# Loading the upper half of an expert weight from GpSimd's queue, and three idle products before a score product, in a fused mLSTM and MLP kernel

## The chip, the cores and the metric

The kernel runs on one core of a Trainium2 chip. A core has a matrix engine (TensorE, PE in the profile; its weight loads are the row PEld), three engines for elementwise work (VectorE or DVE, ScalarE or ACT, GpSimd or POOL), and a SyncE (SP) that does nothing here but issue transfers. Transfers between the chip's memory (DRAM) and the core's working memory (SBUF, 128 partitions) run on 16 DMA engines. Products of PE go to a small memory of their own, PSUM, in eight banks.

The metric is the time of one execution on the device in microseconds (us). A measurement of this kernel tells a difference of about half a per cent from none.

## The reference

Two stages, joined by a reshape. The first is an mLSTM cell, for 4 batches x 8 heads, 768 steps in time and a head width of 40:

```python
m_new  = np.maximum(f_gate[:, :, t] + m, i_gate[:, :, t])
f_stab = np.exp(f_gate[:, :, t] + m - m_new)
i_stab = np.exp(i_gate[:, :, t] - m_new)
C = f_stab * C + i_stab * np.einsum('bhd,bhe->bhde', vt, kt)
n = f_stab * n + i_stab * kt
h_tilde = np.einsum('bhde,bhe->bhd', C, qt)
denom = np.maximum(np.abs(np.einsum('bhd,bhd->bh', n, qt)), 1.0)
y[:, :, t] = sigmoid(o_gate[:, :, t]) * h_tilde / denom
```

Its output, read as 3072 tokens of 320 numbers, goes through an MLP with a leaky ReLU:

```python
h = x @ w_in                    # (3072, 320) @ (320, 2048)
g = np.maximum(0.01 * h, h)
out = g @ w_out                 # (3072, 2048) @ (2048, 320)
```

w_in and w_out arrive as 64-bit floating numbers; all other inputs are 32-bit. The kernel sees the weights as 64-bit words and makes 32-bit numbers of them itself.

## The kernel before

**Chunks and steps.** The 768 times are cut into 6 chunks of 128. A step is one chunk of one batch: step s has chunk s // 4 and batch s % 4, so there are 24. Within a chunk the recurrence is written as products: scores of q and k (`u_scores`), multiplied by a matrix `w` of exponentials of the gates (`spread_first`, `first_exps`, `next_exps`, `prep_mask`, `prep_exp`), times v (`u_values`), divided and gated (`gate`), turned to have channels on partitions (`u_x`), and a state that is carried on (`state`, `state_copy`, `state_next`). When the four steps of a chunk are done, its 512 tokens go through the MLP, in units that `ff_units` lists: `half(j, h)` (line 855) makes two blocks of 128 hidden channels for half of the tokens, `part` (877) sums the second product. From chunk 1 on the MLP runs in another form with fewer products (1019 and 912). The MLP of one chunk and the cell of the next are woven into one order.

**The order of work.** The program is written out by hand for PE, DVE, ACT and POOL: each of these engines does its instructions strictly in the order in which the Python code makes them. SP's transfers have an order of their own: class `Ordered` (line 90) chains every transfer of the first two chunks behind the one before it. `first_chunk` (line 1167) is the hand-written order of chunk 0 (steps 0 to 3) and of the loads that it and chunk 1 need; the loop behind it does the rest.

**The weights' way in.** w_in is loaded in four quarters of 512 columns (`load_weights`, line 236). A quarter has five blocks of 64 rows and stands in SBUF in two halves: partitions 0 to 63 hold the first 256 columns, partitions 64 to 127 the other 256. The order of the blocks is different in the two halves, 0 1 2 3 4 below and 1 2 3 4 0 above (`SLOTS`), so the lower half is one transfer and the upper half two, of four blocks and of one. Quarter 0 is loaded in two parts of 128 + 128 columns (`es`), the quarters 1 to 3 (`WHOLE`) in one. Every transfer of weights is issued by SP. They land as 64-bit words in places that are free for the moment: the quarters 0 and 1 at the end of the hidden activations (`acts`), the quarters 2 and 3 in `raw`. Quarter 0's parts and quarters 1 to 3 come in `first_chunk` and just behind it, between the loads of k, q, v and o of the steps 0 to 5, of a gate matrix that goes through DRAM (`a_dr`), and of w_out, which comes in eight loads over all 128 partitions.

`narrow_weights` (line 278) makes 32-bit numbers of a half quarter in six steps: two on ACT (lines 300, 301) and four on DVE (302, 305, 308, 309). They are taken from generators (`w`, `w1`, `n0`, `n1`) one or two at a time with `run`, so that they stand between other work. ACT's first step waits for the transfers of both halves.

**What POOL does in chunk 0.** Preparing tiles (memsets, `prepare_tiles`, `prepare_step`) and `prep_vu` (540, 544), v multiplied by a gate, which `state` needs. Before the change it issues no transfers.

**Scores of a step.** `u_scores(s)` takes two PSUM banks and makes 8 products of 40 rows from kqT, which ACT or DVE copied out of a transposing product (638); DVE then multiplies them into `w` (651). `warm` (367) and `u_x(1)` (841) hold products of an identity with itself whose results nobody reads.

Of the kernel before, what the change touches and what calls it, by code (L numbers as in the profile page):

```python
# [12 lines left out]
U64 = mybir.dt.uint64  # L13
# [6 lines left out]
def kernel(  # L20
# [26 lines left out]
    nc = tc.nc  # L47
    B, H, S, D = q.shape
    P = 128
# [5 lines left out]
    DP = 64  # L55
# [10 lines left out]
    NF = FF // P  # L66
    GT = B * P
    KF = Dm // P
    KR = Dm - KF * P
    KC = Dm // DP  # L70
# [102 lines left out]
    def prepare_tiles():  # L173

        for u in range(2):
            nc.gpsimd.tensor_copy(cm2[ts(u, SL)], cmask[ts(u, SL), ts(u, SL)])
        nc.gpsimd.memset(xb[:], 0.0)
        for t in rb_t:
            nc.gpsimd.memset(t[:, :, RL:], 0.0)

    def prepare_step(n):

        nc.gpsimd.memset(S_v[n][:SL, 0, :, :, DB:], 2.0)
        nc.gpsimd.memset(S_v[n][SL:, 1, :, :, DB:], 2.0)
        nc.gpsimd.memset(S_t[n][QW:SL, 1], 0.0)
# [3 lines left out]
    QN = NF // 4  # L189
    QC = 4 * P  # L190
# [40 lines left out]
        yield nc.vector.tensor_tensor(t2, a22, a12, op=ALU.subtract)  # L231
        yield nc.vector.tensor_tensor(t4, a21, t2, op=ALU.subtract)

    WHOLE = (1, 2, 3)

    def load_weights(n, es=(0, 1)):

        m = n - QN
        if n < QN:
            dst = w_in[:, n, :]  # L240
        else:
            dst = w_out[:, 2 * m : 2 * m + 2, :].rearrange("p a d -> p (a d)")
        to = dst
        if wide:
            if n < 2:
                at = NF * GT - 2 * WC * (n + 1)
                raw = acts_l[:, at : at + 2 * WC].bitcast(U64)
            elif n < QN:
                raw = raw_t[:, WC * (n - 2) : WC * (n - 1)]
            elif m < 2:  # L250
                raw = w_out[:].rearrange("p f d -> p (f d)")[:, (2 + m) * WC : (3 + m) * WC].bitcast(U64)
            else:
                at = (4, 0, 1, 2, 3, 4)[m - 2] * HW
                raw = raw_t[:, at : at + HW]
            raws[n] = (raw, dst)
            to = raw
        if n < QN:
            src = moe_w_in[:, n * QC : (n + 1) * QC].rearrange("(k p) (r c) -> r p k c", p=DP, r=2)
            halves = to.rearrange("p (e k c) -> p e k c", e=2, k=KC)
            both = to.rearrange("p (k c) -> p k c", k=KC)  # L260
            if n in WHOLE:
                es = es[:1] if es[0] == 0 else ()
            for e in es:
                for r in range(2):
                    at = 0
                    while at < KC:
                        k0, n_k = run_of(r, at)
                        if n in WHOLE:
                            rows, part = both[DP * r : DP * (r + 1), at : at + n_k], src[r, :, k0 : k0 + n_k, :]
                        else:  # L270
                            rows, part = halves[DP * r : DP * (r + 1), e, at : at + n_k], src[r, :, k0 : k0 + n_k, ts(e, P)]
                        sync.dma_start(rows, part)
                        at += n_k
        else:
            rows = moe_w_out[2 * m * P : 2 * (m + 1) * P, :]
            sync.dma_start(to.rearrange("p (a d) -> p a d", d=Dm), rows.rearrange("(a p) d -> p a d", p=P))

    def narrow_weights(n, e=None):

# [220 lines left out]
    def first_exps(ab, s2):  # L500

        w = w_all[:, s2 : s2 + 2].rearrange("p n (m r t) -> p n r m t", r=RG, t=P)
        for r in range(RG):
            nc.scalar.activation(w[:, :, r], ab[r][:], AF.Exp)

    def next_exps(ab, s2):

        for r in range(RG):
            for n in range(2):
                for m in range(H // RG):  # L510
                    h = m * RG + r
                    bh = (s2 + n) * H + h
                    yield nc.scalar.activation(  # L513
                        st[s2 + n]["w"][:, h, :], ab[r][:, n, m, :], AF.Exp, bias=gT[0][:, 0, bh : bh + 1], scale=1.0,
                    )
# [16 lines left out]
    def prep_vu(s):  # L532

        c, b = divmod(s, B)
        d = st[s]
        if s < NS:
            d["vu"] = wk.tile([P, H, 2, V1], F32, name="vu")
            g = gT[c][:, 1, ts(b, H)].unsqueeze(2).unsqueeze(3)
            if c == 0:
                nc.gpsimd.tensor_tensor(  # L540
                    d["vu"][:, :, :, :DB], d["va"][:, :, :D].rearrange("p h (k d) -> p h k d", d=DB),
                    g.to_broadcast([P, H, 2, DB]), op=ALU.mult,
                )
                nc.gpsimd.tensor_tensor(
                    d["vu"][:, :, :, DB], d["va"][:, :, D : D + 2], gT[c][:, 1, ts(b, H)].unsqueeze(2).to_broadcast([P, H, 2]),
                    op=ALU.mult,
                )
            else:
                d["ku"] = d["vu"][:].rearrange("p h k d -> p (h k d)")[:, : H * D].rearrange("p (h d) -> p h d", d=D)
                nc.gpsimd.tensor_tensor(  # L550
                    d["ku"], d["k"][:, :, :D], gT[c][:, 1, ts(b, H)].unsqueeze(2).to_broadcast([P, H, D]), op=ALU.mult,
                )
# [87 lines left out]
    def u_scores(s, between=()):  # L640
        d = st[s]
        kqT, w = d["kqT"], d["w"]
        sc = [psc.tile([P, PR, P], F32, name=f"sc{r}", tag="c") for r in range(2)]
        for j in range(PR):
            for r in range(2):
                rows = slice(DP * r, DP * r + D)
                nc.tensor.matmul(
                    sc[r][:, j, :], lhsT=kqT[rows, 0, ts(j, P)], rhs=kqT[rows, 1, ts(j, P)], start=True, stop=True,
                )
        for r in range(2):  # L650
            nc.vector.tensor_tensor(w[:, r::2, :], w[:, r::2, :], sc[r][:], op=ALU.mult)
            for fn in between if r == 0 else ():
                fn()
# [461 lines left out]
    def run(steps, n=None):  # L1115

        for _ in range(H if n is None else n):
            next(steps, None)
# [48 lines left out]
    def first_chunk():  # L1167

        for n in range(2):
            for i in range(3):  # L1170
                load_first(n, i)
        for n in range(2):
            load_first(n, 3)
        load_weights(0, (0,))
        on_v, on_s = nc.vector.tensor_copy, nc.scalar.copy
        gates(0)
        gates_exp(0)
        load_fi(2)
        warm(6)
        ab = spread_masks()  # L1180
        bu, a, _ = bus[0]
        spread_first(ab, a, bu, 0)
        gates_T(0, bu)
        prep_vu(0)
        first_exps(ab, 0)
        u_transpose(0, (on_v, on_v))
        u_scores(0)
        u_transpose(1, (on_s, on_s))
        ab = spread_masks()
        gates(1)  # L1190
        u_scores(1)
        prep_vu(1)
        prepare_tiles()
        e = next_exps(ab, 2)
        w, w1 = narrow_weights(0, 0), narrow_weights(0, 1)
        n0, n1 = narrow_weights(1, 0), narrow_weights(1, 1)
        ffs = []
        prep_o(0)
        prep_o(1)
        u_values(0)  # L1200
        gate(0)
        spread_first(ab, a, None, 2)
        u_values(1)
        load_first(2, 0)
        load_first(2, 1)
        load_weights(0, (1,))
        load_first(3, 0)
        load_first(3, 1)
        load_first(2, 2)
        load_first(3, 2)  # L1210
        load_first(2, 3)
        load_first(3, 3)
        load_weights(1, (0,))
        load_weights(1, (1,))
        run(e, 6)
        u_x(0)
        gate(1)
        run(w, 2)
        run(w, 4)
        u_x(1)  # L1220
        state(0)
        state(1)
        state_copy(0)
        state_copy(1)
        prepare_step(0)
        prepare_step(1)
        run(e, 2)
        ffs = ff_units(0)
        u_transpose(2, (on_s, on_s))
        run(e, 4)  # L1230
        gates_exp(1)
        run(w1, 2)
        run(e, 4)
        ffs[0]()
        run(w1, 2)
        prep_vu(2)
        prep_vu(3)
        u_scores(2)
        u_transpose(3, (on_v, on_s))
        run(w1, 2)  # L1240
        u_gates(1)
        u_scores(3)
        prep_o(2)
        prep_o(3)
        u_values(2)
        ffs[1]()
        gate(2)
        u_values(3)
        gate(3)
        u_x(2)  # L1250
        state(2)
        u_x(3)
        state(3)
        state_copy(2)
        run(n0, 4)
        state_copy(3)
        run(n0, 2)
        run(n1, 6)
        prepare_step(2)
        prepare_step(3)  # L1260
        return ffs

    E = mybir.EngineType
# [158 lines left out]
```

## Time and profile before

| | |
|---|---|
| median of three runs | 475.43 us (474.78 to 477.28) |
| the profiled execution's own time | 475.09 us |
| span of that execution on the core | 473.3 us |
| busy: PE, PEld | 463.5 us (98%), 418.0 us (88%) |
| busy: DVE, ACT, POOL | 338.6 (72%), 204.1 (43%), 171.3 (36%) |
| transfers issued by SP (queue q1) | 51.20 MB in 121,088 packets |
| transfers issued by ACT (queue q10) | 7.21 MB in 40,128 packets |
| mean granted clock of PE | 0.996 |

The page cuts the span into 40 equal slices of 11.8 us; a digit is the busy share of a slice in tenths. A wait is told as the instruction that waited, an arrow, and what it waited for, with the total, the number of times and the longest. In the timeline a row has its start, its duration, the engine, the line of the program, the operation, the tiles (written <- read), the number of instructions, and in brackets the idle time ahead of it. Matrix products of 32-bit numbers appear as two records each. Where a row names SPq, ACTq or POOLq, it is the time in which that engine issues a transfer and not the time of the transfer.

### The profile page before, as it was taken

To read this page: it belongs to the slowest core of one execution; us is meant where nothing else is said; L and a number is where in the kernel's file an instruction comes from. 1 tells how busy PE (TensorE), PEld (TensorE's weight loads), DVE (VectorE), ACT (ScalarE), POOL (GpSimd) and SP (SyncE) were. 2 spreads that over 40 slices of the span, in tenths; PEclk is the share of its full clock that TensorE was granted. 3 is DMA by queue.
4 is the path that set the end of the run, shared out by engine and by line. 5 is a ranking of instruction groups with operands and counts; after the bars stand their busy time and mean duration, and the time that the engine had idled before them with its cause. 6 is when DMAs were issued, how large, how long until landed. Compare 5 with 4: busy or idle time off the path is not lost.

```text
span 473.3 us, 14138 instructions
## 1 busy us (share of the span) xinstructions
PE 463.5 (98%) x5723; PEld 418.0 (88%) x5723; DVE 338.6 (72%) x607; ACT 204.1 (43%) x497; POOL 171.3 (36%) x205
## 2 busy tenths in 40 slices
PE   7998989999999999999999999999999999999997
PEld 6777878767788899988899988999988999988997
DVE  3868689999679989878688867788847786105531
ACT  3756878755337411367311366311456311253210
POOL 4330577274335154923214923214822005300020
PEclk9989999999999999999999999999999999999999
DMA  9999998886741595965754765753875103100001
GB/s 118 173 176 175 220 193 239 203 173 129 158 132 50 150 166 125 194 141 122 176 121 106 182 133 129 188 115 76 186 153 129 54 25 82 56 1 2 8 8 42
DMA packets 161281, 59.31 MB, mean 125 GB/s; under 512 B 123904, under 2 KB 152640, under 8 KB 161216
## 3 DMA queue, kind: packets, MB, share of 16 engines
q1 hardware_dynamic: 121088, 51.20, 48.7%
q10 hardware_dynamic: 40128, 7.21, 9.3%
q8 instruction: 45, 0.74, 0.7%
q14 instruction: 20, 0.16, 0.1%
HBM read 51.68 MB, written 6.70 MB: 123 GB/s over the span
## 4 chain that ended last, share of the span: by engine, by line
PE 89%; DMA 4%; ACT 3%; DVE 1%; SPq 1%; issue 1%; POOL 0%; DVEq 0%; POOLq 0%; ACTq 0%
PE ph L1019 33%; PE po L912 33%; PE po L877 8%; PE pT L794 3%; PE sd L706 3%; PE ph L855 3%; DMA raw<-in_moe_w_in_dram 3%; DMA acts<-in_v_dram 1%; SPq L96 1%; PE sd L712 1%; PE ab L495 1%; PE hN L766 1%; ACT w L513 1%; PE warm L367 1%; ACT w_in L300 1%
## 5 line engine op out<-in xcount | busy, mean ns | idle before, releaser
L912 PE MATMUL po<-w_out,acts 128*128 128x160 f32 x640 | 89.1, 300 | 0.0
L912 PEld LDWEIGHTS po<-w_out,acts 128*128 128x128 f32 x640 | 87.3, 190 | 0.6 <-ACT acts L1044 0.3
L1019 PE MATMUL ph<-xT,w_in 64*128 64x256 f32 x720 | 82.8, 378 | 0.0
L1019 PEld LDWEIGHTS ph<-xT,w_in 64*128 64x128 f32 x720 | 69.6, 187 | 8.3 <-issue 0.6
L1048 DVE TENSOR_TENSOR acts<-acts,ph 128x512 f32<-128x512 f32 x60 | 38.5, 683 | 40.3 <-PE ph L1019 40.3
L912 PE MATMUL po<-raw,acts 128*128 128x160 f32 x480 | 66.4, 300 | 0.0
L912 PEld LDWEIGHTS po<-raw,acts 128*128 128x128 f32 x480 | 65.4, 190 | 0.3
L1052 ACT COPY acts<-ph 128x512 f32<-128x512 f32 x60 | 32.2, 589 | 49.7 <-PE ph L1019 49.7
L522 POOL TENSOR_TENSOR w<-w,i 128x512 f32<-128x512 f32 x20 | 31.2, 1570 | 53.5 <-DMA w<-a_dr 26.5
L1044 ACT ACTIVATE acts<-acts 128x1024 f32<-128x1024 f32 x30 | 31.6, 1057 | 41.5 <-DVE acts L1048 33.7
L682 POOL TENSOR_TENSOR S<-S,f 40x336 f32<-40x336 f32 x36 | 31.3, 870 | 47.3 <-PE pT L794 31.8
L530 ACT ACTIVATE w<-w,gT 128x64 f32<-128x64 f32 x160 | 41.6, 340 | 12.1 <-DMA a_dr<-a 5.5
L723 DVE TENSOR_TENSOR qn<-w,sd 64x384 f32<-64x384 f32 (+1 forms) x80 | 33.4, 418 | 13.5 <-ACT acts L1052 7.8
L855 PE MATMUL ph<-xT,w_in 64*128 64x256 f32 x320 | 39.5, 395 | 1.1 <-DVE w_in L309 0.8
L855 PEld LDWEIGHTS ph<-xT,w_in 64*128 64x128 f32 x320 | 32.7, 194 | 5.5 <-DVE w_in L309 1.0
L877 PE MATMUL po<-w_out,acts 128*128 128x320 f32 x128 | 36.7, 437 | 0.0
L1019 PE MATMUL ph<-acts,w 64*128 64x256 f32 x320 | 36.3, 379 | 0.0
L808 POOL TENSOR_TENSOR xb<-xb,den 128x320 f32<-128x320 f32 x16 | 11.7, 729 | 67.2 <-DVE xb L805 62.5
L1019 PEld LDWEIGHTS ph<-acts,w 64*128 64x128 f32 x320 | 30.6, 187 | 3.6
L877 PEld LDWEIGHTS po<-w_out,acts 128*128 128x128 f32 x128 | 23.5, 190 | 9.2 <-ACT acts L863 0.3
L950 POOL TENSOR_TENSOR y<-y,raw 128x160 f32<-128x160 f32 x10 | 9.6, 958 | 59.5 <-ACT y L949 59.5
L595 DVE TENSOR_TENSOR qn<-kqT,ea 64x512 f32<-64x512 f32 x32 | 30.0, 938 | 0.8
(179 smaller groups left out, 734.6 us busy)
## 6 DMA issues: line engine op xcount, KB each, us to landing
rb<-in_k_dram SPq DMA_DIRECT2D x64, 80.0 KB
rb<-in_q_dram SPq DMA_DIRECT2D x64, 80.0 KB
rb<-in_o_gate_dram SPq DMA_DIRECT2D x64, 80.0 KB
ea<-a_dr SPq DMA_DIRECT2D x32, 128.0 KB
raw<-in_moe_w_out_dram SPq DMA_DIRECT2D x6, 640.0 KB
w<-a_dr ACTq DMA_DIRECT2D x24, 128.0 KB
x_dr<-x SPq DMA_DIRECT2D x64, 40.0 KB
xT<-x_dr SPq DMA_DIRECT2D x16, 160.0 KB
```

The source lines that it names most:

```text
L522: nc.gpsimd.tensor_tensor(w, w, cm2.unsqueeze(1).to_broadcast([P, H, SL]), op=ALU.add)
L530: yield nc.scalar.activation(w[:, h, :], w[:, h, :], AF.Exp, bias=gT[c][:, 0, bh : bh + 1], scale=1.0)
L595: nc.vector.tensor_tensor(mixed(s)[rows, 1 - r], d["kqT"][rows, 1].rearrange("p (h t) -> p h t", t=SL), d["ea"][rows], op=ALU.mult,)
L682: nc.gpsimd.tensor_tensor(new, old, g, op=ALU.mult)
L723: nc.vector.tensor_tensor(mixed(s)[toks, u, hs], w[toks, hs], bank[1 - u][to[u][hs.start], hs], op=ALU.mult,)
L855: nc.tensor.matmul(ph[r][:, cols], lhsT=w_row(r, slot, j), rhs=xT[DP * r : DP * (r + 1), slot, cols], start=(slot == 0), stop=(slot == KC ...
L877: nc.tensor.matmul(po[n][:], lhsT=acts[:, f, ts(n, P)], rhs=w_out[:, f, :], start=(f == 0), stop=(f == NF - 1),)
L912: nc.tensor.matmul(bank[:], lhsT=left[:, f, :], rhs=right[:, f, :], start=f == 0, stop=f == KH - 1)
L1019: nc.tensor.matmul(bank[r][:, e, :], lhsT=left(r)[rows, e], rhs=right(r)[rows], start=first and e == 0 and m == 0, stop=e == 1 and m == le ...
L1044: nc.scalar.activation(to, z, AF.Prelu, alpha=0.01)
L1048: nc.vector.tensor_tensor(to[:, 2 * r : 2 * r + 2], to[:, 2 * r : 2 * r + 2], bank[r], op=ALU.add)
L1052: nc.scalar.copy(to[:, 2 * r : 2 * r + 2], bank[r])
```

## The change

The upper half of every quarter of w_in is no longer issued by SP but by POOL, with the same two transfers of four blocks and of one (`load_upper`). They stand at written places in POOL's order: the two parts of quarter 0 behind `prep_vu(0)` and `prepare_tiles`, quarter 1 behind `prep_vu(2)`, quarter 2 behind `prep_vu(3)`, quarter 3 behind `prepare_step(3)`, the end of `first_chunk`. SP keeps the lower halves, in their places. `u_scores(3)` begins with three products of the identity with itself, into the first of its two banks, which the score products overwrite. `state_copy(3)` stands ahead of all six steps of `n0` where it stood behind four of them; two of these four are DVE's.

```diff
-    WHOLE = (1, 2, 3)
+    WHOLE, UPPER = (1, 2, 3), (0, 1, 2, 3)
+
+    def raw_of(n):
+
+        if n < 2:
+            at = NF * GT - 2 * WC * (n + 1)
+            return acts_l[:, at : at + 2 * WC].bitcast(U64)
+        return raw_t[:, WC * (n - 2) : WC * (n - 1)]
...
             for e in es:
-                for r in range(2):
+                for r in range(1 if n in UPPER else 2):
...
+    def load_upper(n, e=None):
+
+        src = moe_w_in[:, n * QC + QC // 2 : (n + 1) * QC].rearrange("(k p) c -> p k c", p=DP)
+        if e is None:
+            both = raw_of(n)[DP:].rearrange("p (k c) -> p k c", k=KC)
+        else:
+            both, src = raw_of(n)[DP:].rearrange("p (e k c) -> p e k c", e=2, k=KC)[:, e], src[:, :, ts(e, P)]
+        nc.gpsimd.dma_start(both[:, : KC - 1], src[:, 1:])
+        nc.gpsimd.dma_start(both[:, KC - 1 :], src[:, :1])
...
         sc = [psc.tile([P, PR, P], F32, name=f"sc{r}", tag="c") for r in range(2)]
+        for _ in range(3 if s == 3 else 0):
+            nc.tensor.matmul(sc[0][:, 0, :], lhsT=ident[:], rhs=ident[:], start=True, stop=True)
...
         prep_vu(0)
+        load_upper(0, 0)
...
         prepare_tiles()
+        load_upper(0, 1)
...
         prep_vu(2)
+        load_upper(1)
         prep_vu(3)
+        load_upper(2)
...
         state_copy(2)
-        run(n0, 4)
         state_copy(3)
-        run(n0, 2)
+        run(n0, 6)
         run(n1, 6)
         prepare_step(2)
         prepare_step(3)
+        load_upper(3)
```

More of the change, by code (lines that the diff above doesn't have):

```diff
@@ L244, in load_weights @@
         if wide:
[L245 to L249, printed above, removed]
+            if n < QN:
+                raw = raw_of(n)
             elif m < 2:
```

## The prediction

> **What bounds the kernel now.** The first view is the page's busy shares and slices.
>
> ```profile
> PE 463.5 (98%) x5723; PEld 418.0 (88%) x5723; DVE 338.6 (72%) x607; ACT 204.1 (43%) x497; POOL 171.3 (36%) x205
> ...
> PEclk9989999999999999999999999999999999999999
> DMA  9999998886741595965754765753875103100001
> GB/s 118 173 176 175 220 193 239 203 173 129 158 132 50 150 166 125 194 141 122 176 121 106 182 133 129 188 115 76 186 153 129 54 25 82 56 1 2 8 8 42
> ```
>
> TensorE (PE) works 463.5 of 473.3 us, so the kernel ends sooner only by what PE loses. It loses in two places: in idle, nearly all of it early, and in slice 3 (24 to 36 us), where the granted clock fell. The DMA engines are full in the same 70 us and half empty after. The second view is PE's own waits over the whole span, the third PE's timeline from 20 to 40 us.
>
> ```profile
> PE sc L647 <- DVE kqT L638: 1.7, 2, 0.9
> PE warm L367 <- POOL ident masks.py:199: 1.5, 1, 1.5
> PE sd L712 <- POOL vu L550: 0.9, 1, 0.9
> PE ph L855 <- DVE w_in L309: 0.8, 1, 0.8
> PE tk L621 <- DMA kn<-in_k_dram: 0.8, 1, 0.8
> PE xt L843 <- DVE x L754: 0.5, 1, 0.5
> PE ph L855 <- ACT acts L863: 0.3, 1, 0.3
> PE tk L621 <- DMA rb<-in_q_dram: 0.3, 1, 0.3
> ```
>
> ```profile
> 22.78 2.43 PE L855 MATMUL ph<-xT,w_in 64*128 64x256 f32 x20 [0.77 <-DVE w_in L309]
> ...
> 28.43 1.16 PE L647 MATMUL sc<-kqT 40*128 40x128 f32 x16 [0.75 <-DVE kqT L638]
> 29.52 1.13 PE L741 MATMUL pa<-S,w 128*64 128x41 f32 x32
> 30.58 4.12 PE L855 MATMUL ph<-xT,w_in 64*128 64x256 f32 x20
> ```
>
> The waits end at 70.3 us; from there to the last output PE has no gap. So whatever PE gains before 70 us reaches the end one for one, if nothing swallows it. The last row is the same work as the first and took 4.12 instead of 2.43 us: 1.69 us lost to the clock. The fourth view, windows, gives per stretch the busy time of PE, PEld, DVE, ACT and POOL, then the clock, the DMA share and GB/s.
>
> ```profile
> 14.00:14.50 0.50, 0.50 (x12) 0.47 (x10) 0.47 (x4) 0.10 (x1) 0.50 (x4) 1.00 0.95 324
> 30.50:31.00 0.50, 0.50 (x8) 0.42 (x6) 0.50 (x2) 0.00 (x0) 0.50 (x3) 0.75 1.08 344
> 31.00:32.50 1.50, 1.50 (x10) 1.20 (x8) 1.42 (x6) 0.00 (x0) 1.10 (x4) 0.50 1.08 203
> 37.00:40.00 3.00, 2.64 (x35) 2.30 (x37) 1.76 (x6) 2.17 (x5) 0.00 (x0) 1.00 1.05 196
> 57.50:59.00 1.50, 1.50 (x98) 1.43 (x92) 0.00 (x0) 1.25 (x5) 0.00 (x0) 1.00 1.04 388
> 64.50:65.50 1.00, 1.00 (x13) 0.89 (x11) 0.02 (x1) 0.98 (x3) 0.87 (x2) 1.00 1.01 407
> ```
>
> w_out, loaded over 128 partitions, streams at 388 and 407 GB/s; w_in, loaded over 64 partitions at a time, at 196 and 203 with the engines just as busy. Only where one half ends and the other begins (14.0, 30.5) do w_in's packets reach 324 and 344. So it is the half that is slow, not the source.
>
> **The transfers.** A quarter of w_in is 320 x 512 x 8 bytes, 1.31 MB; four make 5.24 MB. At 200 GB/s they hold the DMA engines 26 us; with both halves in flight at 390 they would hold them 13. Lower halves stay on SP, ten transfers leave it, and everything behind them on SP (k, q, v of steps 2 to 7, the gates' rows, w_out) goes out sooner. One write changes its place on SP: a_dr<-bu (72.17) goes out behind a w_out load (74.61), some 3 us later. Its first reader, ea<-a_dr, goes out at 90.17, so I cost it at nothing.
>
> What PE lost to transfers: 0.76 for kn of step 4 (46.56 us); 0.35 at 52.53 (ACT stood 1.53 us for raw of quarter 2, then was late with L863); 0.28 for rb of step 5 (63.08); 0.95 at 70.33 for vu of step 5, whose chain on POOL began with 7.67 us of waiting for w<-a_dr at L522. Sum 2.34. I let all of it go: at 46 us three quarters are in, 19.7 us of transfer at 200 GB/s, and if half of that overlaps the transfers are some 5 us ahead, more than PE's own lead (1.69 plus what it gained so far, at most 4). What is late next at 70 us is POOL's chain behind DVE's x (L774, 64.07): L779, L780, L559, L682, L550 take 0.72, 0.71, 1.39, 0.89, 0.85, which ends at 68.7, in time for 69.4.
>
> **POOL's new work.** Ten transfers are issued by POOL, and no row shows what one costs it. Nearest rows: SP's issue of the same w_in transfers, 0.61 us at the least, and one of 3.42 us where the queue was full. I take 1.4, between the median 0.62 and the 2.14 that is the longest into acts: 2.8 a pair, 14 in all, where POOL is 36% busy.
> - Upper 0, first half: POOL is free at 9.98; issued by 12.8, 256 KB and 64 KB in 1.6 us, there by 15 to 16; ACT's L300 wants it at 19.00. vu of step 1 moves from 12.83 to 13.8; PE wants it at 20.6.
> - Upper 0, second half: behind prepare_tiles (1.7 us), issued by 18.3, there by 20.5; wanted at 24.52.
> - Upper 1: behind vu of step 2, which waits for v until 27.86 at the latest. Issued by 31.6, 3.2 us of transfer, there by 34.8; wanted at 38.53, or 36.84 without the slow clock. vu of step 3 moves from 30.9 to 33.2; PE wants it at 36.4.
> - Upper 2 by 36.0, there by 41; wanted at 45.59. Upper 3 behind prepare_step(3), by 40, there by 45; wanted at 59.46. POOL's next work, L413, waits until 47.08 in any case.
> All five land in time as long as a pair stays under 4.9 us: 9.98 + d + 0.95 + 1.7 + d + 2 = 24.52, with 1.6 us of transfer in the 2. As bounds: nothing up to there, and at 3.42 each (6.8 a pair) 3.8 us at L300.
>
> DVE shares time with POOL: L309 took 0.83 us alone and 1.68 beside POOL. The second half of upper 0 is written beside gate(0) and gate(1) on DVE (L750 to L755), where PE has 0.2 us to spare. 0 to 1.0 us; I take 0.4.
>
> **The products.** Three 128x128 products at L841's pace (four in 1.06 us) take 0.80 us. They fill the 0.75 us in which PE waits for kqT, and their PSUM bank is free at 27.68, when L651 has read it: 0.05 us more. They also fill the stretch judged before the slow clock. That lasted from 30.75 to 34.16, 3.41 us; the stretch of that length before it held the 0.75 us gap and the thin products of 40 rows and 41 columns. If the filling keeps the clock up, 1.69 go. A gap of 0.77 at 22 us cost no clock, so a gap alone doesn't decide; the thin products do count, and 0.8 us of dense work is 23% of that stretch. The bounds are 0 and 1.69 and I take 1.69.
> The Trainium skill, "TensorE: Matmul & The Clock Gate", the table "Why this matters for your kernels", asks only that no idle of about 3 us stands between bursts. The trace differs: the clock fell behind a gap of 0.75. By that rule the products would keep nothing and the sum would be 473.2.
>
> **state_copy of step 3 ahead of two steps of quarter 1's narrowing.** It takes 0.68 us of DVE's idle 1.12 before L302 (39.37) and leaves L308 0.68 earlier; PE wants that weight at 43.2 and it is done at 42.9. Nothing, and less danger.
>
> **Sum.** The profiled execution took 475.09 (span 473.3 and 1.8 around it), 0.34 below the median 475.43. 475.09 - 2.34 - 1.69 + 0.05 + 0.4 = 471.5.
>
> **Rivals.**
> - Two halves don't overlap. Then transfers end as before, PE arrives 1.69 us sooner and waits that much longer for kn at 46.56: 475.1, or 474.6 because kn no longer stands behind the upper half on SP. For it: the bursts at 14.0 and 30.5 last only half a microsecond. Against it: they reach 324 and 344. The Trainium skill, "SBUF — State Buffer", section "Can I just issue two DMAs to hit both halves?", says no: two such transfers gained 6% over one. By that rule 475; the trace's bursts disagree as far as they go.
> - The clock falls all the same, there or elsewhere, as every arrival shifts: 471.5 + 1.69 = 473.2.
> - Slower: POOL writes its transfers too slowly. Place: L300 at 24.52, where ACT's exponentials and kqT of step 3 stand behind it. From 4.9 us a pair on, twice the excess. At 6.8: upper 0 is 3.8 us late, PE idles and the clock falls once more; 475.09 + 3.8 + 0.4 - 2.34 = 477.0 with a clock loss as before. For it: DVE is busy nearly all the time at 9 to 37 us and POOL's L540 went from 0.72 to 1.40 beside it. Against: it takes four times SP's 0.62. The Trainium skill, "SBUF — State Buffer", section "SBUF: two separate sides", warns that descriptors of a transfer issued by GpSimd can't be written while DVE holds the port they share; no run here shows it yet.
>
> **How the numbers follow.** Forecast 0.57 (own range 470.4 to 472.9), clock falls 0.12, no overlap 0.15, POOL too slow 0.16. A measurement tells about 0.5%, 2.4 us, from no change: faster is below 473.05. Forecast nearly all below (0.54) and half the clock case (0.06): 0.60 faster. The rest of these and no overlap: 0.24. POOL: 0.16. The range runs from 470.0 (the sum without the 0.4 for DVE and without the 0.77 at 22.78, 470.3, and 0.3 for scatter) to 476.0, which leaves out most of the slow case and a little below: 0.2.
>
> **What would show it.** Forecast: GB/s near 350 where quarters 1 and 2 load; no PE wait on kn or rb; clock 1.00 at 30 to 34 us; ph at 30.6 in 2.4 us. Overlap wrong: w_in still at 200 GB/s and kn waiting. POOL wrong: rows on POOL's queue over 2.4 us, and ACT's L300 waiting for transfers at 24 us. What would make the sum wrong is a chain that I call hidden, DVE from 75 to 124 us above all (94% busy), which has 0.7 us on PE at L309 (83.0).

## The result, and the profile after

The changed kernel takes 477.70 us in the median of 20 executions (475.55 to 478.97); the kernel before took 475.62 beside it (473.91 to 477.67, 20 executions). The ratio is 1.0036, with a 95% interval from 1.0025 to 1.0048: slower by a third of a per cent, 1.7 us, less than the half per cent that the prediction set as its bound and clearly not zero. The forecast was 471.5 with a range to 476.0, so it was wrong in sign. The profiled execution of the changed kernel took 477.64 us.

From here on line numbers are those of the changed kernel; what stood at 621, 712 and 855 before stands at 635, 728 and 871. First its page: busy shares, clock and transfers in 40 slices of 11.9 us.

```profile
span 475.8 us, 14162 instructions
...
PE 463.8 (97%) x5729; PEld 417.1 (88%) x5729; DVE 337.6 (71%) x607; ACT 203.8 (43%) x497; POOL 176.9 (37%) x215
...
PEclk9998999999999999999999999999999999999999
DMA  9999999976651584965664765753775203100001
GB/s 123 168 167 215 191 189 235 204 165 131 149 142 36 147 175 113 199 142 120 162 142 91 187 134 126 191 126 71 180 148 118 81 15 84 57 0 2 8 8 41
...
q0 software_dynamic: 800, 2.62, 2.6%
```

PE has the same work as before and a span 2.5 us longer. POOL's queue (q0) moved half of w_in, 2.62 MB, as the change says. The dip of the clock has moved from slice 3 to slice 4. The fourth slice moves 215 GB/s where it moved 175, the fifth 191 where it moved 220; the 350 that two halves in flight were to bring stands nowhere.

PE's waits, and its timeline from the products to step 4:

```profile
PE tk L635 <- DMA kn<-in_k_dram: 1.1, 1, 1.1
PE dC L678 <- issue: 1.1, 1, 1.1
PE sc L663 <- DVE kqT L652: 0.9, 1, 0.9
PE tkq L649 <- ACT xT L860: 0.7, 1, 0.7
...
PE ph L871 <- ACT acts L879: 0.6, 1, 0.6
PE ph L871 <- DVE w_in L323: 0.4, 1, 0.4
```

```profile
29.02 0.94 PE L659 MATMUL sc<-ident 128*128 128x128 f32 x6
29.89 1.16 PE L663 MATMUL sc<-kqT 40*128 40x128 f32 x16
30.98 1.13 PE L757 MATMUL pa<-S,w 128*64 128x41 f32 x32
32.04 2.43 PE L871 MATMUL ph<-xT,w_in 64*128 64x256 f32 x20
...
37.82 0.27 PE L678 MATMUL dC<-vu,kn 128*40 128x42 f32 x3
39.15 0.46 PE L678 MATMUL dC<-vu,kn 128*40 128x42 f32 x13 [1.05 <-issue]
39.54 8.43 PE L871 MATMUL ph<-xT,w_in 64*128 64x256 f32 x60
49.03 0.25 PE L635 MATMUL tk<-ident,kn 64*40 64x64 f32 x2 [1.06 <-DMA kn<-in_k_dram]
```

The products do what was forecast: the MLP's product at 32.04 takes 2.43 us instead of 4.12. But PE is late before that (its first MLP product starts at 23.80 and not at 22.78), and the gain does not last. PE pauses 1.05 us ahead of 39.15, meets a slow clock there, and reaches step 4 at 49.03 where the kernel before reached it at 46.56, still waiting for kn. The waits for vu and rb of step 5, 1.23 us before, are gone, and the lag shrinks to 0.85 us at 76.68 (hN, L782, before at 75.83). Behind that it grows again, to 1.6 at 92 and some 2 at 111. The narrowing of w_out on DVE stands in PE's waits there, and other runs, shown at the end, tell how this goes with the waits that are gone.

The windows, columns as in the prediction (busy times, clock, DMA share, GB/s):

```profile
30.00:32.00 2.00, 2.00 (x48) 1.87 (x48) 1.97 (x4) 0.94 (x2) 1.98 (x4) 1.00 0.96 214
32.00:34.00 2.00, 2.00 (x22) 1.78 (x20) 1.93 (x8) 0.00 (x0) 1.89 (x5) 1.00 1.14 217
34.00:36.00 2.00, 2.00 (x43) 1.61 (x39) 1.30 (x6) 0.72 (x3) 0.85 (x4) 1.00 1.11 202
36.00:38.00 2.00, 1.54 (x27) 1.07 (x24) 1.89 (x6) 1.14 (x4) 1.54 (x3) 1.00 1.07 196
38.00:40.00 2.00, 0.95 (x18) 0.80 (x17) 0.30 (x2) 1.10 (x3) 0.00 (x0) 0.91 1.03 234
40.00:42.00 2.00, 2.00 (x12) 1.61 (x10) 1.89 (x5) 2.00 (x4) 0.00 (x0) 0.50 1.04 281
```

From 30 to 38 us the engines move 196 to 217 GB/s, the pace of one half in the kernel before, and for much of that time only one half is in flight: from 30 to 32 POOL's queue moves nothing, and from 33 to 36 it moves 0.54 of the 0.65 MB. From 38 to 42 both queues carry a half. Their packets, MB and share of the 16 engines in these 4 us:

```profile
q0 software_dynamic: 180, 0.64, 60.8%
q1 hardware_dynamic: 277, 0.39, 42.8%
```

Together that is 258 GB/s: more than one half alone, and far from 390. POOL's own rows, and two of ACT's that stood at 13.63 and 14.53 before with waits of 0.25 and 0.43 us:

```profile
9.37 0.79 POOL L289 DMA_DIRECT2D acts<-in_moe_w_in_dram  x1
10.15 0.54 POOL L290 DMA_DIRECT2D acts<-in_moe_w_in_dram  x1
...
36.38 0.63 POOL L289 DMA_DIRECT2D raw<-in_moe_w_in_dram  x1
37.00 0.54 POOL L290 DMA_DIRECT2D raw<-in_moe_w_in_dram  x1
```

```profile
14.91 0.47 ACT L580 ACTIVATE raw<-raw 128x320 f32<-128x320 f32 x1 [2.15 <-DMA raw<-in_o_gate_dram]
17.52 0.47 ACT L580 ACTIVATE raw<-raw 128x320 f32<-128x320 f32 x1 [2.14 <-DMA raw<-in_o_gate_dram]
```

A pair costs POOL 1.2 to 1.3 us, not 2.8. But behind the first of them SP's small loads of o are late: ACT waits 4.3 us for two of them.

### The profile page after: what moved, and what is told of

The parts are those of the page before. It is cut to its first block, busy times and chain, and to the rows that moved or that the text cites. A ratio compares the mean times of both kernels' runs of the same rounds, so it can differ in the third digit from the quotient of the medians.

```text
span 475.8 us, 14162 instructions
## 1 busy us (share of the span) xinstructions
PE 463.8 (97%) x5729; PEld 417.1 (88%) x5729; DVE 337.6 (71%) x607; ACT 203.8 (43%) x497; POOL 176.9 (37%) x215
## 3 DMA queue, kind: packets, MB, share of 16 engines
q0 software_dynamic: 800, 2.62, 2.6%
## 4 chain that ended last, share of the span: by engine, by line
PE 84%; DVE 7%; ACT 3%; DMA 2%; SPq 2%; issue 1%; POOL 1%; DVEq 0%; POOLq 0%
PE ph L1035 33%; PE po L928 32%; PE po L893 4%; PE pT L810 3%; PE sd L722 3%; PE ph L871 2%; SPq L96 2%; DVE w_out L322 1%; DVE w_out L323 1%; DVE w_out L316 1%; DMA w<-a_dr 1%; DVE w_out L319 1%; DVE qn L739 1%; ACT w L527 1%; PE pa L757 1%
## 5 line engine op out<-in xcount | busy, mean ns | idle before, releaser
L536 POOL TENSOR_TENSOR w<-w,i 128x512 f32<-128x512 f32 x20 | 31.1, 1564 | 49.6 <-DMA w<-a_dr 45.6
L1060 ACT ACTIVATE acts<-acts 128x1024 f32<-128x1024 f32 x30 | 31.6, 1055 | 40.5 <-DVE acts L1064 32.3
```

The source lines that it names most:

```text
L536: nc.gpsimd.tensor_tensor(w, w, cm2.unsqueeze(1).to_broadcast([P, H, SL]), op=ALU.add)
L1060: nc.scalar.activation(to, z, AF.Prelu, alpha=0.01)
```

## Experiments

Two theories were set against each other. Theory A: the time up to step 4 is set by when SP's small loads land; a transfer that POOL puts beside or ahead of them takes the engines from them, and what PE gains is waited out there. Its rivals: it is the half, or POOL's issuing, or the products, wherever they stand. Every ratio below is to the kernel before on the same chip, with its 95% interval.

**The products alone.** The kernel before with the three products:

```diff
         sc = [psc.tile([P, PR, P], F32, name=f"sc{r}", tag="c") for r in range(2)]
+        for _ in range(3 if s == 3 else 0):
+            nc.tensor.matmul(sc[0][:, 0, :], lhsT=ident[:], rhs=ident[:], start=True, stop=True)
```

> The kernel before with the three idle products alone. Theory A (transfers bound the first 60 us, so what PE gains before 46 us is waited away at kn of step 4): the slow clock at 31 to 34 us goes, PE reaches step 4's transposes 1.7 us sooner and waits 1.7 us longer there; time within 1 us of before. Theory B (the clock's 1.7 us reach the end): 473.9, 1.7 us under before. Theory C (the products do harm): over 476.5.

475.81 us, ratio 0.9994 (0.9970 to 1.0017). PE's timeline:

```profile
30.68 2.43 PE L857 MATMUL ph<-xT,w_in 64*128 64x256 f32 x20
...
46.02 0.25 PE L621 MATMUL tk<-ident,kn 64*40 64x64 f32 x2 [1.26 <-DMA kn<-in_k_dram]
```

The clock stays full and the 1.69 us are there. At step 4 PE waits 1.26 us for kn instead of 0.76, with a wait of 0.46 for DVE on the way, and is 0.54 us ahead of the kernel before, no more; its span ends 0.6 earlier. (The profiled execution was the fastest of the 12, 474.44.) The kernel before says the same without any edit, as its clock falls in most executions and not in all: of 92 in these studies, the 18 with a mean granted clock of 0.999 or 1.000 had a median of 475.1 us, the 71 from 0.992 to 0.996 one of 476.1 (three stood at 0.989). So a full clock goes with some 1 us, not with 1.69. With the products alone 9 of 12 executions had 0.999 or more.

**The transfers alone.** The changed kernel without the three products.

```diff
-        for _ in range(3 if s == 3 else 0):
-            nc.tensor.matmul(sc[0][:, 0, :], lhsT=ident[:], rhs=ident[:], start=True, stop=True)
```

> The changed kernel without the three products. Theory A (the 2 us lost are the transfers', through SP's loads that arrive later): 477 to 479, as the changed kernel or up to 1.5 us slower as the clock falls at the scores of step 3 again. Theory C (the products do the harm): 475.6, as before.

477.08 us, 1.0013 (0.9989 to 1.0037): the transfers alone bring no gain either. PE's wait for kn is 1.7 us, and step 4 begins at 48.59. None of 12 executions had a mean clock of 0.999 or more; with the products added, the changed kernel, it was 5 of 20. Those 5 had a median of 476.7 us, against the 475.1 of the kernel before at a full clock: the change is slower at equal clock too.

**The rates by themselves.** Three kernels that move data without computing; they give one profile each. The first:

> This kernel computes nothing: it only moves data, in nine stretches of 2.62 MB with a pause between (the eighth 5.24 MB), and writes zeros as the output. Theory A (the two halves of w_in don't overlap, whoever issues them): lower halves alone, halves in turn on SP, halves on SP and POOL at once, and on SP and ACT at once all run at 190 to 230 GB/s; w_out over 128 partitions at about 400. Theory B (they overlap, and in the changed kernel something else held the rate down): SP with POOL, and SP with ACT, at 350 or more. The fifth stretch, SP alternating blocks of 64 rows of the lower and the upper half, tells whether a fine mixture on one queue reaches the 324 to 396 GB/s seen for half a microsecond at the turn from one half to the other: above 300 if so, about 210 if not. In the last but one, 16 loads of k on SP beside four upper halves on POOL: by A the loads of k end later by a good part of the 13 us that the upper halves take alone.

The second and third:

> This kernel only moves data in and writes zeros; the whole computation is left out. Six stretches, one after the other: w_in over all 128 partitions in rows of 4 KB (2.62 MB, SP alone); a lower half on SP beside another lower half on POOL; ten k loads of 160-byte rows on SP alone; the same ten beside four upper halves on POOL; the same ten beside four w_out loads on POOL; four w_out loads on SP alone. The half is slow (what the prediction said): w_in over 128 partitions goes near w_out's 380 to 410 GB/s, and two transfers into the same 64 partitions stay near 205 where SP beside POOL into different halves gave 265. The source is slow: w_in over 128 partitions stays near 205 to 265. For SP's small loads: if a queue of rows of 2 KB takes the engines' time packet by packet, k falls to about 46 GB/s beside the upper halves, as in the first rates kernel, and about as low or lower beside w_out (rows of 2,560 bytes). If it is half-partition transfers that hold the engines, k beside w_out keeps more than 100 of its 167 GB/s.

> This kernel only moves data in and writes zeros; the whole computation is left out. Stretches, one after the other, each begun only when all of the one before has landed: ten k loads of 160-byte rows on SP alone; the same beside four upper halves of w_in on POOL; the same beside four upper halves on ACT; the same beside four w_out loads on POOL; four lower halves on POOL beside four upper halves on SP; four lower halves on POOL alone. Theory A (a second queue with rows of 2 KB or more takes the engines from rows of 160 bytes, whoever issues it): k goes at 40 to 70 GB/s beside uppers on POOL, the same beside uppers on ACT, and the same or less beside w_out. Rival one (it is POOL's kind of queue): beside ACT's uppers k keeps more than 100 of its 167 GB/s. Rival two (it is transfers into 64 partitions): beside w_out k keeps more than 100. The two halves together go at about 265 GB/s, a half on POOL alone at about 205, as a half on SP did.

| in flight | mean GB/s |
|---|---|
| w_in, lower halves, SP alone (first kernel, 22 to 31 us) | 215 |
| w_in, lower half, then upper, SP alone (first, 49 to 57) | 222 |
| w_in, lower halves, POOL alone (third, 206 to 214) | 213 |
| lower and upper by turns in blocks of 64 rows, SP alone (first, 121 to 130) | 202 |
| two lower halves, SP and POOL (second, 36 to 41) | 228 |
| lower on SP, upper on POOL (first, 74 to 81) | 248 |
| lower on SP, upper on ACT (first, 99 to 105) | 268 |
| lower on POOL, upper on SP (third, 174 to 182) | 286 |
| w_in over all 128 partitions, SP (second, 19 to 24) | 360 |
| w_out over all 128 partitions, SP (first, 147 to 152) | 379 to 412 |

So it is the half that is slow and not the source: w_in over 128 partitions goes at 360. Its rows are 4 KB there and not 2, but that isn't the reason, as POOL's packets into one half are 3.4 KB on average (503 for 1.70 MB) and go at 213. Two halves in flight do not add up: 248 to 286, not 390. In the row with blocks by turns the engines were busy only 76% of the time, so it settles nothing. The Trainium skill, "SBUF — State Buffer", section "Can I just issue two DMAs to hit both halves?", says 6% for two concurrent transfers; alone on the chip these runs show 15 to 34%, and in the changed kernel 258 beside the 214 of one half (30 to 32 us) is 21%.

The third kernel also has what the prediction never asked: ten k loads of 160-byte rows on SP's queue (q1), alone and beside other queues. The lines are its transfer view (queue, packets, MB, share of the 16 engines) from 28 to 36 us, alone; from 57 to 67 beside four upper halves on POOL, and 62 to 67 of these by themselves; from 97 to 107 beside the same on ACT (q10), and then 106 to 108; from 138 to 146 beside w_out on POOL.

```profile
q1 hardware_dynamic: 9429, 1.49, 112.1%
...
q0 software_dynamic: 544, 1.84, 89.6%
q1 hardware_dynamic: 1652, 0.26, 19.9%
...
q0 software_dynamic: 315, 1.03, 96.6%
q1 hardware_dynamic: 321, 0.05, 10.5%
...
q10 hardware_dynamic: 646, 1.20, 65.1%
q1 hardware_dynamic: 4160, 0.66, 55.6%
...
q10 hardware_dynamic: 188, 0.35, 103.0%
q1 hardware_dynamic: 53, 0.01, 3.4%
...
q0 software_dynamic: 536, 2.50, 82.4%
q1 hardware_dynamic: 1680, 0.27, 19.6%
```

Alone, k moves 1.49 MB in 8 us, 186 GB/s, and a load lands 3.8 us after its issue. Beside POOL's upper halves it moves 0.26 MB in 10 us, 26 GB/s, and lands after 13.7 us. Beside ACT's it keeps 66, beside w_out on POOL (0.27 MB in 8 us) 34. Both rivals fall. The half is not needed, as w_out does it too. And it is not POOL's kind of queue: the 66 beside ACT is a mean over times when ACT's queue had little in it (ACT issued its fourth transfer only at 103.61, POOL all eight by 58.8). While ACT's queue is full, from 106 to 108, k moves 0.01 MB in 2 us, no more than beside POOL. Every queue of long rows that was tried takes the engines from one of short rows.

The Trainium skill, "DMA: Bandwidth & Descriptors", section "Queues, rings and completion order", says that a DMA engine takes turns between its queues by whole packets. The trace agrees where POOL's queue is full all the time: from 62 to 67 us it moves 315 packets and k 321. As POOL's are some 20 times as large (1.03 MB to 0.05), k is left with 10 GB/s. Over the whole stretches, with their gaps, the bytes are 7 to 1 beside POOL and 1.8 to 1 beside ACT.

The first kernel had k beside POOL's upper halves too: 46 GB/s from 182 to 192 us, 16.5 us from issue to landing. In the second kernel k hardly ran beside w_out, so that stretch told nothing.

**Quarter 3's upper half back on SP; quarter 0's back on SP; both.** Three kernels from the changed one:

```diff
-    WHOLE, UPPER = (1, 2, 3), (0, 1, 2, 3)
+    WHOLE, UPPER = (1, 2, 3), (0, 1, 2)
...
-        load_upper(3)
```

The second has `UPPER = (1, 2, 3)` and drops `load_upper(0, 0)` and `load_upper(0, 1)`; the third has `(1, 2)` and drops all three.

> The changed kernel with quarter 3's upper half back on SP; the other three quarters stay on POOL. Theory A (POOL's upper half of quarter 3 takes 0.655 MB, 3.2 us at 200 GB/s, ahead of k, v and w of step 4): kn of step 4 lands about 3 us sooner, its wait of 1.06 us goes, and the time falls by 1 to 2.5 us to 475 to 476.7. Theory D (what was lost was lost before 40 us, by quarters 0 and 1): no change, 477.7.

> The changed kernel with both parts of quarter 0's upper half back on SP; quarters 1 to 3 stay on POOL. Theory A (a queue of 2 KB rows takes about three quarters of the DMA engines' time from SP's 160-byte rows, so every upper half delays the small loads that are in flight with it): the delays of o of steps 0 and 1 and of q of step 3 go, ACT's 4.3 us of waiting for o falls under 1, PE's first MLP unit starts at 22.8 instead of 23.8; kn of step 4 is late as in the changed kernel, at 48 to 49 us, because quarter 3's upper half still runs ahead of it. Time 476.5 to 477.7. Theory D (the loss before 40 us is what reaches the end): 475.6 to 476.2.

> The changed kernel with only the quarters 1 and 2 on POOL, 0 and 3 back on SP. Theory A: neither the early loads nor step 4's are passed by more than they were before, step 4's transposes start by 46.5 us and the time is 475 to 476.3, as before; by the prediction's own theory (halves in flight together go at 390 GB/s) it would be 472 to 473.

| on POOL | us | ratio | wait on kn, step 4 |
|---|---|---|---|
| 0, 1, 2, 3 (the change) | 477.70 | 1.0036 (1.0025 to 1.0048) | 1.1 at 49.03 |
| 0, 1, 2 | 476.65 | 1.0008 (0.9987 to 1.0030) | none |
| 1, 2, 3 | 476.03 | 1.0017 (0.9998 to 1.0036) | 2.1 at 47.58 |
| 1, 2 | 474.91 | 0.9992 (0.9974 to 1.0010) | none |

By the ratios quarter 3 costs 0.28% (1.3 us) and quarter 0 0.19% (0.9 us). These single steps are not clear of noise, as their intervals touch. The two together are: the intervals of the first and the last row lie apart, by 0.44% between their middles. The second row's 476.03 lies in the range of the rival (lost before 40 us) and not in theory A's, though kn is late there as A said; with these intervals it decides for neither.

The last row is two kernels in one. Its six executions with a full clock took 473.7 us in the median, where the kernel before took 474.8 (five executions on that chip); the six others took 476.4, where it took 475.5. So with a full clock this version seems some 1 us faster, but the clock is full in only half of its executions. Six against five are a hint and no more.

With quarter 3 on SP the wait for kn is gone (its profile has one of 2.5 us for q of an earlier step, with the clock down at 24 to 31 us; that of the last row, its slowest execution, has a slow clock at 29 to 36, products or not). With quarter 0 on SP, ACT's o of the steps 0 and 1 come in one row after 0.40 us of waiting, at 13.24:

```profile
13.24 0.98 ACT L580 ACTIVATE raw<-raw 128x320 f32<-128x320 f32 x2 [0.40 <-DMA raw<-in_o_gate_dram]
```

**More of quarter 3 ahead of step 4.** The lower half of quarter 3 goes to POOL's queue too, in the same place:

```diff
-                for r in range(1 if n in UPPER else 2):
+                for r in range(0 if n == 3 else 1 if n in UPPER else 2):
...
+        if n == 3:
+            low = moe_w_in[:, n * QC : n * QC + QC // 2].rearrange("(k p) c -> p k c", p=DP)
+            nc.gpsimd.dma_start(raw_of(n)[:DP].rearrange("p (k c) -> p k c", k=KC), low)
```

> The changed kernel with quarter 3's lower half issued by POOL too, right behind its upper half: twice the bytes ahead of step 4's loads. Theory A: kn of step 4 lands 2 to 3.5 us later still, step 4's transposes start at 51 to 52.5 us instead of 49.0, and the time is 479 to 480.5. Theory D: no change, 477.7.

481.34 us, 1.0118 (1.0101 to 1.0136). The waits of PE and the row:

```profile
PE tk L638 <- DMA kn<-in_k_dram: 7.2, 1, 7.2
```

```profile
52.34 0.33 PE L638 MATMUL tk<-ident,kn 64*40 64x64 f32 x2 [7.21 <-DMA kn<-in_k_dram]
```

A half of a quarter, 0.655 MB, at 200 GB/s is 3.3 us of transfer. With one half ahead of it step 4 starts at 49.03 (47.58 with quarter 0 on SP) instead of 46.56, with a second at 52.34, 3.3 us later. The time rises by 3.6 us in the medians, clear of noise and above the range that theory A gave. The clock is at 0.5 from 47 to 58 us in this profile, behind the start of the long wait, which may be the rest.

**The same half, later.** Quarter 3's upper half stays on POOL's queue, with the same instructions, but behind the mask of step 4 (L536, 46.83), which stands behind a copy that waits for v of step 4. Quarter 0 is on SP, so the run to compare is the one with 1, 2 and 3 on POOL.

```diff
-        load_upper(3)
...
                         prep_mask(B)
+                        load_upper(3)
```

> Quarter 0 whole on SP again; quarters 1 and 2 as changed; quarter 3's upper half on POOL, but behind POOL's mask of step 4, at about 50 us and so behind the landing of the small loads of step 4. Theory A (what hurts is the transfer put ahead of the small loads of step 4): the wait on kn at step 4 is 0 to 1 us, and the time is that of the run with the quarters 1 and 2 alone on POOL, 0.998 to 1.000 of the kernel before (474.5 to 475.5). Rival (it is POOL's issuing, or the half as such, wherever it stands): as the run with quarter 0 back on SP, 1.0017 (476.2). If the late half is late for its reader at about 59 us, PE shows a wait on w_in of quarter 3 at 60 to 66 us, and the time is above 476.

475.23 us, 0.9987 (0.9974 to 1.0001), where the early place had 1.0017. PE's timeline around step 4, and its waits:

```profile
43.79 2.43 PE L871 MATMUL ph<-xT,w_in 64*128 64x256 f32 x20 [1.85 <-DVE w_in L323]
46.15 0.25 PE L635 MATMUL tk<-ident,kn 64*40 64x64 f32 x2
```

```profile
PE ph L871 <- DVE w_in L323: 2.6, 2, 1.9
```

Issued at 48.05 the half delays no load that PE waits for: the wait for kn is gone, and step 4 begins at 46.15 instead of 47.58. This kernel issues three of the four upper halves on POOL, as the early one does, and is no slower than the kernel before, while the change (from 1.0025) lies outside its interval. So POOL's issuing as such isn't what costs.

What the place of this one half is worth at the end is not settled. The medians differ by 0.30% (1.4 us), but the intervals overlap at their ends. The two profiled executions, both with a full clock, have spans of 473.0 (early) and 473.1 us (late): the 1.43 us that PE is ahead at step 4 are gone at the `hN` products of step 5, which begin at 74.60 (early) and 74.80 (late), as PE stands 0.59 us at step 5's transposes and 0.33 for vu, among others, on the way. The clock is full in 10 of 12 executions here and in 6 of 12 with the early place, and a good part of the 1.4 may be that. What stands in the way before step 4 is 2.6 us for quarter 1's weights, which are late.

**Quarter 1 on SP as well.** If those 2.6 us came from POOL's queue they should go. From the kernel just shown:

```diff
-    WHOLE, UPPER = (1, 2, 3), (1, 2, 3)
+    WHOLE, UPPER = (1, 2, 3), (2, 3)
...
-        load_upper(1)
```

> As the run with quarter 3's upper half late, but quarter 1 whole on SP too; only quarter 2 in its changed place on POOL, and quarter 3 behind POOL's mask of step 4. In the run before this one PE waited 2.6 us for quarter 1's weights at 36 to 44 us. If that wait came from quarter 1's upper half landing late on POOL's queue, it falls below 1 us here and the time is 0.995 to 0.998 of the kernel before (473.7 to 475.2). If it came from SP's own pace of bytes, the wait stays near 2.6 and the time is that of the run with the quarters 1 and 2 alone, 0.998 to 1.001.

476.38 us, 1.0005 (0.9991 to 1.0018): neither theory. The wait for w_in falls to 1.1 us, and others come in its place.

```profile
PE ph L871 <- ACT acts L879: 1.1, 1, 1.1
PE ph L871 <- DVE w_in L323: 1.1, 2, 0.8
PE tk L635 <- issue: 1.0, 1, 1.0
...
PE tk L635 <- DMA kn<-in_k_dram: 0.5, 1, 0.5
```

**The order on SP instead.** The kernel before with the products, nothing on POOL, but kn of step 4 ahead of quarter 2, and the loads of step 5 ahead of quarter 3 and of the first w_out.

```diff
-        load_weights(2)
...
+        load_weights(2)
...
-        load_weights(3)
-        load_weights(QN + 0)
...
+        load_weights(3)
+        load_weights(QN + 0)
```

> No transfers on POOL: the kernel before with the three products, and with two changes of SP's order: k of step 4 goes out ahead of quarter 2, and q, v, w, k and o of step 5 ahead of quarter 3 or of the first load of w_out. Theory A (before 60 us the order in which bytes pass the DMA engines decides, and 160 KB ahead of 1.3 MB costs the big load under 1 us): kn's wait of 1.3 us and the wait for vu at 70 us go, 473.5 to 474.8. If the products' 1.7 us can't be had by order either: 475.8 as with the products alone.

477.63 us, 1.0039 (1.0020 to 1.0057), slower, against what I had priced for the large loads put back.

```profile
PE ph L857 <- ACT acts L865: 2.6, 2, 2.5
```

kn is there (step 4 at 45.27), but now a quarter is late: ACT stands in order at its narrowing, the hidden activations behind it, and PE behind those. At these bytes a load that comes forward puts another one back, whoever issues it. No version beat the kernel before by more than its interval.

## Why the prediction was wrong, by its own steps

- **"With both halves in flight they would hold them 13."** This is the step that failed first. 5.24 MB at the 248 to 286 GB/s of the rate kernels are 18 to 21 us. In the kernel the pace was 196 to 217 from 30 to 38 us, and 258 from 38 to 42, where both halves were in flight. The bursts of 324 and 344 that it was read from last half a microsecond; a rate read from half a microsecond is none for thirteen. The reading that the half and not the source is slow was right.
- **"At 46 us ... the transfers are some 5 us ahead."** A term was missing here altogether: what POOL's transfers do to SP's loads. Quarter 3's upper half went out at 36.38, where SP still had kn, v and w of step 4 to move. At 200 GB/s it is 3.3 us of transfer; kn came 2.47 us later, at 49.03, instead of 5 earlier. Moving that half behind those loads let step 4 begin 1.4 us sooner. Quarter 0's halves did the same to o at 15 to 17 us. With both quarters back on SP the 0.44% are gone, and with a second half ahead of kn 0.8% are added, both clear of noise: the sign of the result comes from this term. How it divides between the two quarters, and between waits and the clock, is open.
- **The 2.34 us of waits.** The 0.95 for vu and 0.28 for rb went, as forecast. The 0.76 for kn became 1.06, the 0.35 at 52.53 became 0.56 at 55.20. And what went at vu did not reach the end, as the bullet on DVE shows.
- **"If the filling keeps the clock up, 1.69 go."** The mechanism was right in most executions (9 of 12 with the products alone kept the clock, against 18 of 92 without). In the changed kernel it was 5 of 20. The step was mis-sized, since it counted the gain at the end, and kn and DVE take most of it back: with the products alone 0.54 us is left at step 4. In the changed kernel's profile the clock then fell at 40 us (0.50), behind the 1.05 us pause and thin products. The 60 products there took 8.43 us; before, with small waits among them, 7.31, and 6.75 where the clock is full and nothing holds them (the run with 0, 1 and 2 on POOL).
- **The products, 0.05.** Nearly right: they take 0.94 us where the gap was 0.75, so some 0.2 more and not 0.05, and the row of waits for kqT fell from 1.7 to 0.9.
- **POOL, 2.8 a pair.** Over-sized: 1.2, beside a DVE that is nearly always busy. The slower rival that rested on it fell: POOL issues in time, and that the rival's 477.0 lies near the measured 477.7 is chance, as the reason is another. What was under-sized is the way from issue to landing, 9.0 us in the median for the five larger transfers. Quarter 1's upper half was issued by 30.1, sooner than the 31.6 of the forecast, and was to be there by 34.8; ACT waited 0.90 us for it, until 39.31. The Trainium skill, "SBUF — State Buffer", section "SBUF: two separate sides", warned of writing descriptors while DVE holds the shared port; these rows, 0.53 to 0.79 us each, show no such stall in the issuing; when the descriptors were written no view tells.
- **"Two halves don't overlap."** This rival had the mechanism of the first step nearly right, and its 474.6 took kn to come sooner "because kn no longer stands behind the upper half on SP". It stood behind the upper half on POOL instead.
- **DVE from 75 to 124 us.** Named as what would make the sum wrong, and it did: the lag of 0.85 us at 76.68 grew to some 2 there, with `w_out L323` among PE's waits. The other runs tell part of it. From the `hN` at 75 us to the next one PE takes 14.93 us in the kernel before and with the products alone, which both wait some 1 us for vu ahead of it. It takes 15.71 or 15.72 in the changed kernel, without the products, with quarter 3 back, with quarter 0 back and with all of quarter 3 ahead, which don't wait for vu, though they get there anywhere between 74.60 and 81.45; the other four runs lie between 15.12 and 15.66. So of the 0.95 won at vu 0.78 are lost again, and PE's waits in the changed kernel's profile name DVE there. The wait for vu had given DVE time to catch up. What adds the rest of the 2 us was not taken apart.
- **Not settled.** The 0.4 for DVE beside POOL and the move of `state_copy(3)` were not measured alone. The 1.05 us that PE's timeline puts down to "issue" at 39.15 has no cause that the profile shows; the late version, with the same move, has no such pause there.

## What to carry to other kernels

A second queue adds little to the pace here (248 to 286 GB/s for two halves against 213 to 222 for one); above all it re-orders the transfers. Before a large load goes to another queue, list the small loads that are to land in the same microseconds, and charge them its bytes. A clock or a wait that is won ahead of another wait is worth only what that wait leaves over; look for the next wait first, and go on with it to the end of the span. And take a rate from a stretch as long as the one it is to be used for.

## What the runs showed of the hardware

A queue of 160-byte rows that has 186 GB/s alone keeps 26 beside upper halves on POOL's queue (46 in another kernel, and 10 while that queue is always full), 66 beside them on ACT's with its gaps (some 4 while it is full), and 34 beside w_out on POOL's. Their sum stays near 200 (beside w_out: near 350). Two transfers into the two halves of the partitions reach 248 to 286 GB/s, two into the same half 228, one 213 to 222, and one over all 128 partitions 360 to 412. A transfer of 256 or 512 KB costs POOL 0.63 to 0.79 us to issue and one of 64 or 128 KB 0.53 to 0.56, about what SP's rows show.
